# All low parts of the usual experts' weights on VectorE, products by low parts last in a block, and the split's steps at the block's begin and end

## The chip, the cores and the metric

One core of a Trainium2 chip. The engines run their own queues in order and wait for each other by semaphores: TensorE (PE; its weight loads, PEld, overlap its products), VectorE (DVE), ScalarE (ACT), GpSimd (POOL) and the DMA queues, of which SyncE (SP) issues most. The metric is the device time of one execution in microseconds (us).

## The reference

Attention over pooled queries, then two mixtures of experts (MoE), each with 8 experts of which a token takes one:

```python
# attention: 2 batches, 8 heads, 1152 keys, queries averaged in pairs, head size 64
x = softmax(scale * mean_of_pairs(q) @ k.T) @ v            # -> 1152 tokens of 512
# first MoE: expert = argmax(x @ w_gate); an expert takes its first 288 tokens
out[token] = gate * (relu(x[token] @ w1[e]) @ w2[e])       # w1 512x1024, w2 1024x512
# second MoE: tokens with x @ w_skip > 0 only, no limit
out[token] = x[token] + gate * (relu(x[token] @ w1[e]) @ w2[e])
```

All data are float32.

## The kernel before

Attention takes the first 318 us and is left alone by the change, but for its tail. Then come the experts of the first MoE (344 to 519 us), its last block beside the second router (to 565 us), and the experts of the second MoE.

**Split numbers.** For the experts a float32 is split into a high and a low part of twelve bits each (`hi`, `lo` for weights; `xx[:, 0]`, `xx[:, 1]` for tokens; `hh`, `hl` for hidden values), and a product is the sum of three: high by high, high by low, low by high. An expert's weights are 2 x 4096 numbers on each of 128 partitions. `split_ops` returns 17 steps for them: step u casts piece u (512 columns) of `raw` to `hi` on ACT (line 818) and subtracts for piece u-1, `lo = raw - hi` (line 808). The subtraction ran on POOL for the pieces in `ON_POOL`, 6 of 16, and in some splits for further ones (`pool_steps`), else on DVE. After the last piece of a quarter, `load_next` has SP load a quarter of a later expert's weights (1 MB) into the place that came free; for the second half of an expert these loads are issued behind its last chunk (`late`).

**A block.** `block_t` computes one chunk of up to 128 tokens of an expert: `first(0)` (12 products of 128x128 by 128x512, into `ph`), relu on ACT to `hs` (line 942), `first(1)` with the transposes `turn(0)` in its middle (to `pg`; ACT copies to `hh`, line 950; DVE subtracts to `hl`, line 951), `second(py, 0)` with `turn(1)` in its middle, `second(py, 1)`; then DVE scales to `yt` (lines 991, 993), makes an index `ix`, and POOL scatters the rows. Between the parts `flush(list, n)` issues the next n steps of a list: `fill` is the split of the next expert's weights, `preps` the transposes (`psx`, line 913) and the two parts of the next chunks' tokens: `xxn` for the next expert, `xx` for this one's second chunk. A main block is an expert's first chunk; it alone carries `fill`. The second and third chunks stand under conditions (`tc.If`, lines 1172 and 1178) on the count of tokens. An engine that skips them runs a branch and then raises its own semaphore by what the skipped instructions would have added; whoever waits for an instruction from the far side of the condition waits for that. `hs` is written by DVE too, in `block_h` (up to 64 tokens), under a condition.

**Order.** The order of issue on each engine is that of the calls in the code (`manual_schedule`); nothing reorders it. In the first MoE the last expert's main block is left for the end: there `fill` holds five empty steps, then router steps mixed with the split of the second MoE's first expert, whose `hi` and `lo` go to the places of the weights that this block itself uses. Tiles of `wp` have two places each for the halves, in two pools that the experts take in turn.

Of the kernel before, what the change touches and what calls it, by code (L numbers as in the profile page):

```python
# [8 lines left out]
F32 = mybir.dt.float32  # L9
F32R = mybir.dt.float32r  # L10
BF16 = mybir.dt.bfloat16
# [5 lines left out]
P = 128  # L17
# [4 lines left out]
def fused_kernel(  # L22
# [21 lines left out]
    KD = DM // P  # contraction chunks of the first product  # L44
    KF = F // P  # and of the second
    KC = S // P  # key chunks
    QP = 96  # rows of a chunk of queries, as loaded
    QC = SQ // QP
    CH = [P] * (SQ // P) + ([SQ % P] if SQ % P else [])  # token chunks of a batch
    NCH = len(CH)  # L50
    NT = B * NCH
    ROW = DM + 8  # a dispatched row: the token, its gate, its index
    REG = N  # rows of an expert's region
    NPRE = 3  # chunks of an expert that are read without an index
# [8 lines left out]
    # ---------------------------------------------------------------- constants  # L63
# [6 lines left out]
    rev = consts.tile([P, NT, E], F32, name="rev")  # E - e  # L70
# [10 lines left out]
    tri = consts.tile([P, P], BF16, name="tri")  # tri[k, m] = 1 where k < m  # L81
# [9 lines left out]
    def load_small(zeros):  # L91
        """Steps: the routers' weights, the capacity, zeros where tokens may be missing."""
# [22 lines left out]
        def capacity_value():  # L115
            # low + 2^32 * (high + (low < 0)), and not below 0
# [12 lines left out]
    # ---------------------------------------------------------------- weights  # L129
    RW = KD * F // 2  # words of a partition in one load: half of w1[e] or of w2[e]  # L130
# [15 lines left out]
    # ---------------------------------------------------------------- routing  # L146
# [5 lines left out]
    def masks(m):  # L152
        """1 in the rows of an expert's chunks that have no token."""
        nc.vector.tensor_tensor(
            out=mask[m],
            in0=cnt[m].unsqueeze(2).to_broadcast([P, E, NPRE]),
            in1=rowid.unsqueeze(1).to_broadcast([P, E, NPRE]),
            op=ALU.is_le,
        )

    def route(sp, ps_r, lg, nt, gate_out, prev, do=None, half_rows=()):
        """Three steps: the expert of each token, one-hot; its place among that expert's tokens; its gate.

        lg [P, nt, >= E] in SBUF; prev: one-hots of earlier tokens. The dictionary that is returned gets
        the one-hots (oh), the place (rank) and the first row of the expert's region (base).
        """
# [74 lines left out]
    def together(*lists):  # L241
        """The steps of several lists in turn."""
# [6 lines left out]
    def logits(m, rows, lg, ta, tb, xt, lt, groups, on_scalar=lambda j: j and j % 2, j0=0):  # L249
        """Steps to the logits of chunks of 128 tokens: for each group of chunks (each in a quadrant of the  # L250
        partitions) the transposes, the product and the way back."""
# [36 lines left out]
    def in_line(groups):  # L288
        """The steps of logits() in a row, a group's last ones behind the first transpose of the next."""
# [6 lines left out]
    def add_rows(ps, rows, places, first, last):  # L296
        """Adds to ps the transpose of the rows, each in its place: exact, by products with 0 and 1."""
# [10 lines left out]
    def places_of(place, oh):  # L308
        """One-hots of the tokens' places among an expert's first 128."""
# [3 lines left out]
    def count(ps_r, ohs, limit, m):  # L313
        """Tokens of each expert, on every partition, and in row 0 as integers."""
# [11 lines left out]
    def warm(ps, n):  # L326
        """Products that nobody reads: the array's clock would fall while it waits."""
# [24 lines left out]
    # ================================================================ attention  # L352
# [10 lines left out]
    def gate(b, ta, tb, groups):  # L363
        """Routing of a batch's tokens, and their rows to their experts' regions: steps to the logits, and the rest."""
# [31 lines left out]
    with ExitStack() as actx:  # L396
# [16 lines left out]
        PARTS = [(0, 2), (2, NCH)]  # chunks of the two halves of a pair's product with v  # L413
# [24 lines left out]
        def split0(n):  # L438
            """Sums of the pairs of queries, as far as the loads allow ahead."""
# [898 lines left out]
```

## Time and profile before

| | us |
|---|---|
| median of 3 runs | 742.46 |
| the runs | 737.96 to 743.23 |
| span of the profiled execution, first to last instruction | 734.7 |

The profiled execution has no time of its own beside its span; a run counts some us around the span. Shares of busy time are averages over attention, the routers and the experts.

### The profile page before, as it was taken

The numbers are of one execution on the slowest core, as the hardware profiler recorded it, in microseconds if no ns is written. First come the engines' busy times: TensorE is split into PE (matmuls) and PEld (weight loads), VectorE is DVE, ScalarE is ACT, GpSimd is POOL, SyncE is SP. The second block draws the span as 40 slices with busy tenths as digits, with TensorE's granted clock in tenths as the row PEclk, the third lists the DMA queues.
The fourth block names the chain that finished last, engine by engine and source line by source line (L and its number), as shares of the span: only waits on it lengthen the run. The fifth ranks groups of instructions, "written<-read, shape, count | busy, mean of one in ns | idle before, by whom it ended". The sixth has DMA issues, their size and how long they took to land. (4 is left out here: it accounts for less than half of the span.)

```text
span 734.7 us, 11243 instructions
## 1 busy us (share of the span) xinstructions
PE 666.5 (91%) x3978; PEld 485.9 (66%) x3978; DVE 450.1 (61%) x729; ACT 433.3 (59%) x961; POOL 257.3 (35%) x240
## 2 busy tenths in 40 slices
PE   7999999999999999988888998899769888888994
PEld 6766667666767666646666766676648666666673
DVE  5755656565656664564888548842175788888211
ACT  5876767676757676651777347722350677776210
POOL 4322222222222520053566226510165566665010
PEclk8999999999999999999999999999988999999998
DMA  6042624050202122033889618850454798884100
GB/s 179 31 138 104 212 104 167 17 196 17 81 17 82 67 71 78 16 123 114 302 314 331 246 35 311 278 201 19 147 186 147 259 318 303 315 302 162 32 30 13
DMA packets 55599, 111.39 MB, mean 152 GB/s; under 512 B 5470, under 2 KB 14686, under 8 KB 55488
## 3 DMA queue, kind: packets, MB, share of 16 engines
q1 hardware_dynamic: 52128, 102.27, 40.8%
q0 software_dynamic: 3360, 7.72, 2.8%
q8 instruction: 59, 0.97, 0.5%
q14 instruction: 52, 0.43, 0.2%
HBM read 93.51 MB, written 19.71 MB: 154 GB/s over the span
## 5 line engine op out<-in xcount | busy, mean ns | idle before, releaser
L808 POOL TENSOR_TENSOR lo<-raw,hi 128x512 fp32r<-128x512 f32 x101 | 142.0, 1409 | 115.6 <-ACT hi L818 113.2
L808 DVE TENSOR_TENSOR lo<-raw,hi 128x512 fp32r<-128x512 f32 x155 | 157.2, 1065 | 4.3 <-ACT hi L818 4.3
L818 ACT CAST hi<-raw 128x512 fp32r<-128x512 f32 x256 | 141.5, 626 | 0.6 <-PE py L958 0.6
L527 PE MATMUL s_ps<-kop,qop 128*128 128x384 f32 x480 | 125.5, 369 | 1.7 <-ACT a L571 1.4
L555 DVE TENSOR_REDUCE m<-s_ps 128x1 f32<-128x1152 f32 x72 | 97.7, 1357 | 24.6 <-PE s_ps L527 22.4
L601 PE MATMUL pt<-ident,a 128*128 128x128 f32 x648 | 109.8, 283 | 3.2 <-ACT kop L476 1.1
L571 ACT ACTIVATE a<-s_ps,m 128x384 f32<-128x384 f32 (+1 forms) x144 | 106.8, 747 | 3.1 <-DVE m L555 2.9
L476 ACT COPY at<-pt 128x384 f32<-128x384 f32 x144 | 68.2, 481 | 64.0 <-PE pt L601 63.9
L601 PEld LDWEIGHTS pt<-ident,a 128*128 128x128 f32 x648 | 71.5, 140 | 45.9 <-ACT at L476 13.0
L627 PE MATMUL pv<-at,vr 128*64 128x320 f32 (+1 forms) x576 | 97.9, 428 | 0.0
L938 PE MATMUL ph<-hi,xxn 128*128 128x512 f32 x224 | 77.1, 405 | 13.1 <-PEq L1172 10.4
L476 DVE COPY at<-pt 128x384 f32<-128x384 f32 x72 | 39.8, 553 | 76.2 <-PE pt L601 74.1
L951 DVE TENSOR_TENSOR hl<-pg,hh 128x512 fp32r<-128x512 f32 x42 | 28.9, 687 | 89.0 <-ACT hh L950 89.0
L958 PE MATMUL py<-hi,hl 128*128 128x512 f32 x168 | 67.8, 404 | 12.5 <-DVE hl L951 12.5
L942 ACT ACTIVATE hs<-ph 128x512 f32<-128x512 f32 x42 | 25.1, 598 | 91.0 <-PE ph L938 52.3
L527 PEld LDWEIGHTS s_ps<-kop,qop 128*128 128x128 f32 x480 | 75.1, 187 | 5.3 <-ACT a L571 3.8
L958 PE MATMUL py<-hi,hh 128*128 128x512 f32 x168 | 68.7, 409 | 0.6
L886 POOL DMA_INDIRECT out_dram<-yt,ix x23 | 22.6, 981 | 133.0 <-DVE ix L883 81.7
L958 PE MATMUL py<-lo,hh 128*128 128x512 f32 x168 | 67.7, 403 | 0.0
L466 POOL TENSOR_TENSOR qhl<-qr,qhl 96x384 fp32r<-96x384 f32 x30 | 29.9, 1016 | 95.7 <-DVE qhl L464 95.7
L938 PEld LDWEIGHTS ph<-hi,xxn 128*128 128x128 f32 x224 | 42.1, 188 | 27.3 <-ACTq L1172 12.1
L454 POOL TENSOR_TENSOR khl<-kr_None,khl 128x576 fp32r<-128x576 f32 x14 | 19.8, 1414 | 87.2 <-DVE khl L453 87.2
(170 smaller groups left out, 948.2 us busy)
## 6 DMA issues: line engine op xcount, KB each, us to landing
raw<-in_moe_w_dram SPq DMA_DIRECT2D x64, 1024.0 KB, 6.0
x<-xs SPq DMA_DIRECT2D x36, 260.0 KB, 6.3
xs<-xtok SPq DMA_DIRECT2D x8, 780.0 KB, 7.4
qr<-in_q_dram SPq DMA_DIRECT2D x16, 288.0 KB, 3.2
vr<-in_v_dram SPq DMA_DIRECT2D x8, 576.0 KB, 6.0
kr_None<-in_k_dram SPq DMA_DIRECT2D x7, 576.0 KB, 5.0
out_dram<-xtok SPq DMA_DIRECT2D x3, 768.0 KB, 7.7
x<-out_dram SPq DMA_DIRECT2D x4, 512.0 KB, 6.3
```

The lines of the kernel that those rows point to most:

```text
L466: sub.tensor_tensor(out=t[:, 1, :, r, :], in0=qs, in1=t[:, 0, :, r, :].bitcast(F32), op=ALU.subtract)
L476: (nc.vector.tensor_copy if on_vector else nc.scalar.copy)(dst, src)
L527: i = nc.tensor.matmul(s_ps[0:M, bank[j], 0 : 3 * P], qop[n + r][:, part, o : o + M], kop[n + r][:, j, :], start=(part == 0 and r == (c == ...
L555: i = nc.vector.tensor_reduce(out=nm, in_=s_ps[:, lo : lo + 3, 0 : 3 * P], axis=AX.XY, op=ALU.max, negate=True)
L571: i = nc.scalar.activation(a[:, a0 : a0 + nb, :], s_ps[:, b0 : b0 + nb, 0 : 3 * P], AF.Exp, bias=nm, accum_out=t[:, c, n % 2, k : k + 1],)
L601: nc.tensor.transpose(ps[:, x * P : (x + 1) * P], a[:, g, x * P : (x + 1) * P], ident)
L627: nc.tensor.matmul(hold["pv"][j * D : (j + 1) * D, 0:w], vrt[i][:, j, c * D : (c + 1) * D], at_t[2 * i + j, part][:, c, :], start=(c == 0) ...
L808: eng.tensor_tensor(out=lo, in0=raw, in1=hi.bitcast(F32), op=ALU.subtract)
L818: nc.scalar.copy(hi, raw)
L938: lambda d=d, i=i, a=a, b=b: nc.tensor.matmul(ps, xx[:, a, d, :], w1[b][:, d, s], start=(d + i == 0), stop=(d == KD - 1 and i == 2))
L951: nc.vector.tensor_tensor(out=hl[:, fs, :], in0=ps, in1=hh[:, fs, :].bitcast(F32), op=ALU.subtract)
L958: lambda f=f, i=i, a=a, b=b: nc.tensor.matmul(py, a[:, f, :], w2[b][:, f, :], start=(f + i == 0), stop=(f == KF - 1 and i == 2))
```

## The change

1. `ON_POOL` goes. Low parts are on DVE but for `pool_steps`: pieces 13 to 15 of the very first split and 8, 9, 10, 13, 14 of the second MoE's first. The other 14 splits have none on POOL.
2. In `block_t` the loops of `first` and `second` are exchanged: four products high by high, four high by the weights' low part, four low by high, where it was three for each of four pieces.
3. The 17 steps of `fill` are spread as 4 ahead of `first(0)`, then 2, 1, 1, 2, 3 and the rest (4), where it was 2, 3, 2, 2, 3 and the rest (5).
4. Comments are removed; lines behind 788 move up by one to the flush that is added in `block_t`.

```diff
-        NU = 16  # steps of a split
-        ON_POOL = (0, 3, 6, 8, 11, 14)  # those whose low parts GpSimd takes
+        NU = 16
...
-                eng = nc.gpsimd if u in ON_POOL or u in pool_steps else nc.vector
+                eng = nc.gpsimd if u in pool_steps else nc.vector
...
-                for d in range(KD):
-                    for i, (a, b) in enumerate(((0, 0), (0, 1), (1, 0))):
+                for i, (a, b) in enumerate(((0, 0), (0, 1), (1, 0))):
+                    for d in range(KD):
                         mms.append(
...
-                for f in range(hf * 4, hf * 4 + 4):
-                    for i, (a, b) in enumerate(((hh, 0), (hh, 1), (hl, 0))):
+                for i, (a, b) in enumerate(((hh, 0), (hh, 1), (hl, 0))):
+                    for f in range(hf * 4, hf * 4 + 4):
                         mms.append(
...
+            flush(fill, 4)
             mms, relu = first(0)
             flush(mms, 12)
             relu()
             flush(fill, 2)
             mms, relu = first(1)
             flush(mms, 6)
             turn(0)
-            flush(fill, 3)
+            flush(fill, 1)
             flush(mms, 12)
             relu()
-            flush(fill, 2)
+            flush(fill, 1)
             py = pa([P, DM], "py")
             mms = second(py, 0)
             flush(mms, 6)
             turn(1)
             flush(preps, 1)
             flush(fill, 2)
             flush(mms, 12)
             mms = second(py, 1)
             flush(fill, 3)
             flush(mms, 4)
             flush(preps, 1)
             flush(fill, len(fill))
             flush(mms, 12)
```

DVE in the second expert's main block (`lo_2_*` is the split for the third expert, `hl` the hidden values' low part, `xx` a second chunk's), before:

```order
L951 TENSOR_TENSOR hl<-pg,hh 128x512
L808 TENSOR_TENSOR lo_2_0_4385<-raw_2_0_0_3895,hi_2_0_4384 128x512 x2
L808 TENSOR_TENSOR lo_2_0_4385<-raw_2_0_1_3933,hi_2_0_4384 128x512 x2
L951 TENSOR_TENSOR hl<-pg,hh 128x512
L918 TENSOR_TENSOR xxn<-psx,xxn 128x512
L808 TENSOR_TENSOR lo_2_0_4385<-raw_2_0_1_3933,hi_2_0_4384 128x512
L808 TENSOR_TENSOR lo_2_1_4387<-raw_2_1_0_4380,hi_2_1_4386 128x512 x2
L918 TENSOR_TENSOR xx_4393<-psx,xx_4393 128x512
L808 TENSOR_TENSOR lo_2_1_4387<-raw_2_1_1_4382,hi_2_1_4386 128x512 x3
L991 TENSOR_SCALAR yt<-py,x_1_0_3841 128x512
```

and now:

```order
L807 TENSOR_TENSOR lo_2_0_4385<-raw_2_0_0_3881,hi_2_0_4384 128x512 x4
L807 TENSOR_TENSOR lo_2_0_4385<-raw_2_0_1_3933,hi_2_0_4384 128x512
L950 TENSOR_TENSOR hl<-pg,hh 128x512
L807 TENSOR_TENSOR lo_2_0_4385<-raw_2_0_1_3933,hi_2_0_4384 128x512 x2
L950 TENSOR_TENSOR hl<-pg,hh 128x512
L917 TENSOR_TENSOR xxn<-psx,xxn 128x512
L807 TENSOR_TENSOR lo_2_0_4385<-raw_2_0_1_3933,hi_2_0_4384 128x512
L807 TENSOR_TENSOR lo_2_1_4387<-raw_2_1_0_4380,hi_2_1_4386 128x512 x4
L917 TENSOR_TENSOR xx_4393<-psx,xx_4393 128x512
L807 TENSOR_TENSOR lo_2_1_4387<-raw_2_1_1_4382,hi_2_1_4386 128x512 x4
L991 TENSOR_SCALAR yt<-py,x_1_0_3841 128x512
```

Five low parts stand ahead of the first `hl`, two between the two `hl` where there were four, and nine behind the second where there were six.

PE from the second transposes of the same block on (`lo_1_1` is the low part of this expert's second weights), now; before, `hi,hh`, `lo,hh` and `hi,hl` followed each other product by product, in the same places around `pg` and `psx`:

```order
L957 MATMUL py<-hi_1_1_3847,hh 128x512 x4
L957 MATMUL py<-lo_1_1_3848,hh 128x512 x2
L947 MATMUL pg<-ident,hs 128x128 x4
L912 MATMUL psx<-ident,x_2_0_3849 128x128 x4
L957 MATMUL py<-lo_1_1_3848,hh 128x512 x2
L957 MATMUL py<-hi_1_1_3847,hl 128x512 x4
L957 MATMUL py<-hi_1_1_3847,hh 128x512 x4
L912 MATMUL psx<-ident,x_1_1_3851 128x128 x4
L957 MATMUL py<-lo_1_1_3848,hh 128x512 x4
L957 MATMUL py<-hi_1_1_3847,hl 128x512 x4
```

The products that read `hl` moved from third to ninth in each half.

ACT in the last block of the first MoE (`hi_0_0_8738` is the first half of the second MoE's first expert, `gx` a router's transposes), before:

```order
L942 ACTIVATE hs<-ph 128x512
L950 CAST hh<-pg 128x512
L942 ACTIVATE hs<-ph 128x512
L818 CAST hi_0_0_8738<-raw_0_0_0_6697 128x512 x2
L950 CAST hh<-pg 128x512
L261 COPY xT_0_8802<-gx_0_8797 128x512
```

and now:

```order
L941 ACTIVATE hs<-ph 128x512
L817 CAST hi_0_0_8738<-raw_0_0_0_6683 128x512
L949 CAST hh<-pg 128x512
L817 CAST hi_0_0_8738<-raw_0_0_0_6683 128x512
L941 ACTIVATE hs<-ph 128x512
L261 COPY xT_0_8788<-gx_0_8783 128x512
L949 CAST hh<-pg 128x512
```

A cast that waits for PE moved from behind the second `hs` to between the first `hs` and the first `hh`.

## Rows read from the trace of the kernel before

**Rows 1.** The page's first lines: span, then busy us (share) xinstructions

```profile
span 734.7 us, 11243 instructions
...
PE 666.5 (91%) x3978; PEld 485.9 (66%) x3978; DVE 450.1 (61%) x729; ACT 433.3 (59%) x961; POOL 257.3 (35%) x240
```

**Rows 2.** PE's waits from 344 us on: engine, line, releaser; us, times, longest

```profile
PE py L958 <- DVE hl L951: 12.5, 13, 1.4
...
PE pr L214 <- DVE oh L198: 6.0, 2, 5.7
```

**Rows 3.** Timeline of PE, a main block: start us, us, what, [idle before <-releaser]

```profile
446.70 0.47 PE L938 MATMUL ph<-hi,xxn 128*128 128x512 f32 x1 [1.01 <-PEq L1172]
...
450.98 0.60 PE L948 MATMUL pg<-ident,hs 128*128 128x128 f32 x4
...
456.93 0.40 PE L958 MATMUL py<-lo,hh 128*128 128x512 f32 x1
458.25 0.51 PE L958 MATMUL py<-hi,hl 128*128 128x512 f32 x1 [0.92 <-DVE hl L951]
...
462.42 0.47 PE L938 MATMUL ph<-hi,xxn 128*128 128x512 f32 x1 [1.13 <-PEq L1172]
```

**Rows 4.** Timeline of DVE, the same block

```profile
449.04 0.74 DVE L991 TENSOR_SCALAR yt<-py,x 128x512 f32<-128x512 f32 x1
...
452.28 0.69 DVE L951 TENSOR_TENSOR hl<-pg,hh 128x512 fp32r<-128x512 f32 x1 [2.43 <-ACT hh L950]
452.89 4.70 DVE L808 TENSOR_TENSOR lo<-raw,hi 128x512 fp32r<-128x512 f32 x4
457.51 0.68 DVE L951 TENSOR_TENSOR hl<-pg,hh 128x512 fp32r<-128x512 f32 x1
```

**Rows 5.** Timeline of ACT, the same block

```profile
450.02 0.60 ACT L942 ACTIVATE hs<-ph 128x512 f32<-128x512 f32 x1 [3.49 <-DVEq L1172]
450.51 1.13 ACT L818 CAST hi<-raw 128x512 fp32r<-128x512 f32 x2
...
455.22 0.60 ACT L950 CAST hh<-pg 128x512 fp32r<-128x512 f32 x1
```

**Rows 6.** Line 808: engine, operation, count, ns min/median/max, first and last start

```profile
L808 DVE TENSOR_TENSOR lo<-raw,hi x155: 674/681/1806, 318.0 to 677.9; 128x512 fp32r<-128x512 f32 x155
L808 POOL TENSOR_TENSOR lo<-raw,hi x101: 1252/1317/1830, 317.5 to 675.5; 128x512 fp32r<-128x512 f32 x101
```

**Rows 7.** Timelines of DVE, then of POOL, around 448 us

```profile
447.83 1.28 DVE L808 TENSOR_TENSOR lo<-raw,hi 128x512 fp32r<-128x512 f32 x2
...
450.12 0.99 POOL L886 DMA_INDIRECT out_dram<-yt,ix  x1 [2.76 <-DVEq L1172]
```

**Rows 8.** Timeline of PE at the head of two second chunks

```profile
408.25 0.74 PE L938 MATMUL ph<-hi,xx 128*128 128x512 f32 x2 [0.60 <-DVE xx L918]
...
676.20 0.68 PE L1036 MATMUL ph<-hi,xx 128*64 128x512 f32 x2 [0.61 <-DVE xx L918]
```

**Rows 9.** Timeline of PE in attention's tail

```profile
319.84 0.41 PE L653 MATMUL px<-ident,xu 128*128 128x128 f32 x2 [1.60 <-DVE xu L637]
```

**Rows 10.** Timeline of ACT in the last block of the first MoE

```profile
525.35 0.59 ACT L950 CAST hh<-pg 128x512 fp32r<-128x512 f32 x1 [1.45 <-PE pg L948]
526.70 0.60 ACT L942 ACTIVATE hs<-ph 128x512 f32<-128x512 f32 x1 [0.77 <-PE ph L938]
```

**Rows 11.** Timeline of DVE in the second router

```profile
539.27 5.45 DVE L1236 TENSOR_SCALAR do<-lg 128x5 f32<-128x5 f32 x1
```

**Rows 12.** Timeline of POOL in the second router

```profile
539.77 4.92 POOL L808 TENSOR_TENSOR lo<-raw,hi 128x512 fp32r<-128x512 f32 x4
```

**Rows 13.** Two blocks: stretch, us, busy per engine, PE clock, DMA share, GB/s

```profile
377.13:391.84 14.71, 13.63 (x64) 10.38 (x65) 12.21 (x15) 10.84 (x21) 8.74 (x7) 1.00 0.95 332
629.47:645.07 15.60, 13.66 (x64) 10.40 (x65) 13.02 (x17) 11.52 (x22) 9.30 (x8) 1.00 0.92 308
```

**Rows 14.** The page's DMA issues: queue, count, size, median us to landing

```profile
raw<-in_moe_w_dram SPq DMA_DIRECT2D x64, 1024.0 KB, 6.0
```


## Prediction

> **What bounds the kernel now.** I read the page first: TensorE (PE) is busy in 91% of the span [rows 1], so only what makes it wait can pay. The change touches the experts, so I listed PE's waits from 344 us on [rows 2]. At the top stand 13 waits, 12.5 us in all, of the second product for `hl`, the low part of the hidden values that VectorE (DVE) makes. There is one in 13 of the 14 main blocks that also split the next expert's weights; the fourteenth, the first of all, doesn't have it.
>
> One such block in order of time [rows 3 to 5], with 0 at its first product (446.70): 18 products take 4.28 us, 0.24 each; the second transpose gives `hh` at +8.5, done at +9.1; `hl` needs only that, but starts at +10.8, because DVE is still at low parts of weights. PE issues a product at 456.93 and the next at 458.25: 1.32 us where 0.24 is usual, so a stall costs 1.08.
>
> Why is DVE late? A low part takes 674 ns at the least, 681 in the median and 1806 at the most on DVE, 1317 on GpSimd (POOL) [rows 6]. The two lows at 447.83, while POOL stands still (it idles 2.76 us up to 450.12), take 1.28 us together, 0.61 from start to start [rows 7]; the four from 452.89, with POOL at the same kind of work, 4.70 [rows 4]. So the six steps that POOL takes off DVE are paid by DVE in the others. At the start of a block DVE idles 2.43 us before the first `hl` [rows 4] and ACT 3.49 us before `hs` [rows 5]: there is room where the change puts the steps.
>
> **The change part by part.** My sum is made against the profiled execution, whose span is 734.7 us [rows 1]; the runs stand at 738.0 to 743.2, so 3 to 9 us lie around the span, and I take the differences off the median, 742.46.
>
> *Low parts on DVE, 16 of an expert in place of 10.* 16 times 0.61 is 9.8 us; four of `hl` and `xx` at 0.61, and 0.98 from the start of `yt` to the `hs` that waits for the branch behind it [rows 4, 5], make 13.2 in a block that lasts 15.72 now: it fits. Where it lies decides. From `hh` at +9.1 DVE now has `hl`, the `xx` of the next block, five lows, `xx` of the second chunk, four lows: 12 steps of 0.61, 7.3 us, so `yt` at +16.4. `hl` is ready at +9.8. In the new order of products it is wanted six products and one set of transposes later than before: +10.5 plus 1.4 plus 0.4, +12.3. There are 2.5 us of room, and the stall goes. All 13: 12.5 us of idle, and 0.16 each of lost pace (1.08 less 0.92), **-14.6**.
>
> *What is late next.* `hs` of a block's first half waits for DVE to be through its tail and the branch: in the block shown ACT's 3.49 us end on DVE's branch, 0.98 us after the start of `yt` [rows 4, 5]. In the new order that is +17.4, and the next block starts at 15.72 - 1.08 = +14.6, so `hs` could go at +2.8. PE's first 12 products end at about +3.1, and the transposes want `hs` (0.6 long) by +4.28, so it may start as late as +3.7. It is hidden with 0.9 us to spare; what is queued behind `hs` on ACT (`hi` casts, `hh`) has the same room. A slip beyond costs PE one for one. I put **+1.0** for all blocks, 0 to +6.
>
> [...] The trace has the next low start 0.61 us after the one before, while one is recorded as 0.68 long [rows 6, 7]. [...]
>
> *The order of products.* Their number and that of weight loads stays. The low part of the tokens (`xx`, on DVE) is wanted by the ninth product instead of the third. It made PE wait 0.60 and 0.61 at the head of two second chunks [rows 8]; six products are 1.4 us, both waits go: **-1.2**. A gain is bounded by these two rows, a loss I see none: low parts of weights were needed second, now fifth.
>
> *Casts at the begin, on ACT.* Four `hi` casts (two take 1.13 us [rows 5], four about 2.2) now stand ahead of `hs`, in the 3.49 us that ACT idled. They need PE to be through with the expert before, which is so at the block's start, and the load of the weights, below. Nothing as long as they end by +3.7: they end at +2.2.
>
> *The first split, in attention's tail.* Five low parts move from POOL to DVE. PE waited 1.60 us for `xu` there [rows 9], which stood behind one low beside POOL's; now it stands behind two at 0.61. Between +0.6 (one low more in the way) and -1.6 (the wait gone) I take the middle, **-0.5**.
>
> *The last block of the first MoE.* It runs with the split of the second MoE's first expert, whose places are those of its own weights. A placeholder list kept these steps behind the first product; with four steps flushed at the begin the first cast now stands between `hs` and `hh` on ACT and waits for PE to end the first product. `hh` ran at 525.35 and the second half's `hs`, which follows that end, at 526.70 [rows 10]. The cast goes at 526.7 and `hh`, 0.5 behind it, at 527.2, 1.85 later than now, done at 527.8. PE stands still from the first product's end, just before 526.7, less some 0.4 that a group of four router transposes, moved ahead, fills (four took 0.60 with their overlap [rows 3]). **+1.0**, from 0 (other waits hide it) to +1.9.
>
> *The second router.* A tiny DVE step, `do`, takes 5.45 us [rows 11], as long as POOL's four lows in a row at 539.77, 4.92 us [rows 12]; PE stands 5.7 us behind it [rows 2]. One of the four (step 11) goes to DVE, behind this chain: 4.92/4 = 1.2 less, and 0.6 on DVE later. **-0.6**, from -1.2 to +0.6.
>
> Loads: they are started when a quarter's low parts are done; none is added. Scatters on POOL start earlier in the queue and nothing waits for them inside a block.
>
> Sum: -14.6 + 1.0 - 1.2 - 0.5 + 1.0 - 0.6 = -14.9, so 742.46 - 14.9 = 727.6, rounded to 727.5. **I forecast 727.5 us.**
>
> **The rivals.**
>
> *Half of it comes (0.17, 734).* The stall goes, but another pace takes over. The DMA engines are busy 92% of 15.60 us in one block, 14.4 us; another ran 14.71 us at 95%, 14.0 [rows 13]. A block of 14.6 would have them at 96 to 98%, and whatever they can't follow PE gives back. For it: hardly any slack. Against: 95% was held without PE waiting for a weight. At 0.6 us back in each of 13 blocks, +7, so 734.
>
> *A slower kernel: `hs` behind casts that wait for weights (0.06, 752).* The first cast moves from +3.8 to 0. Its quarter is loaded when the fourth low is done, at about +2.9 + 4 x 0.61 = +5.3 of the block before, 9.3 us ahead of the cast; a load takes 6.0 us from issue to landing in the median [rows 14]. The casts may slip to +1.5, so loss starts at a landing of 10.8 us; every us more costs 13 us, and from 12.0 on the gain is eaten. At 12.7 it is 727.5 + 25 = 752. For it: the engines near 96%. Against: it needs double the present landing.
>
> *It doesn't do what it says (0.07, 741).* What holds DVE up may be more than POOL. If lows come 0.77 us apart with POOL silent, 16 x 0.77 + 3.4 = 15.7 fills the present block and DVE sets its length; then the head waits and a little more are left, -1 to -2. Against: 674 ns at the least, 681 in the median, and 0.61 from start to start [rows 6, 7].
>
> *DVE steps don't overlap (0.03, 729).* If each step waits for the recorded end of the last, 12 x 0.07 = 0.9 us puts `hs` at +3.7, just at its limit; 0.1 in each of 13 blocks on the sum as it stands, 729. [...] Against: the starts in rows 7.
>
> **How the numbers follow.** The forecast has 0.67. About 1%, 7.4 us, is what a measurement of this kernel tells from no change (its three runs spread over 5.3): the bounds are 735.0 and 749.9. Faster: nearly all of 0.67, the 0.03, and a little over a third of the half case, 0.76. Same: the rest of the half case, the 0.07 and some of the forecast's edge, 0.17. Slower: 0.07. The range: best case -14.6 - 1.2 - 1.6 + 0 - 1.2 is -18.6, 723.9, and a run at the low edge of the spread, 4.5 lower, 719; upward the half case with its spread to 738. What lies outside is the 0.07 at 741, the 0.06 and a few hundredths below.
>
> **What the new profile would show.** Right: POOL's lows fall from 101 to 8, DVE's rise to 248 with a mean near 0.68 us; no PE wait for `hl`; main blocks without a second chunk at about 14.6 us from start to start; `hs` still ended by DVE's branch, near +2.8; the last block of the first MoE about 1 us longer at `hh`. Wrong if PE waits for `hs` in most blocks, if ACT waits for `raw` at the first cast, if DMA stands at 100%, or if DVE's lows stay at 1 us.

## The result, and the profile after

| | median, us | runs, us | ratio to the kernel before, 95% interval |
|---|---|---|---|
| kernel before | 742.85 | 737.96 to 743.39 (4) | |
| changed kernel | 716.66 | 712.63 to 723.73 (4) | 0.965 [0.961, 0.970] |

The changed kernel is faster by 3.5%, 26 us. I had forecast 727.5 us, 15 us less, with a range from 719 to 738: the direction was right, the gain too small, and the time lies under the range. The ratio leaves out the slowest of the four runs, which is over 1.5% above the fastest; in e8 below the same kernel ran from 715.60 to 724.46 us.

The profiled execution is shorter by 19.6 us (734.7 before [rows 1]). The page's first lines, span and then busy time of each engine:

```profile
span 715.1 us, 11137 instructions
...
PE 660.8 (92%) x3978; PEld 487.7 (68%) x3978; DVE 446.7 (62%) x822; ACT 436.1 (61%) x961; POOL 128.4 (18%) x147
```

POOL went from 35% to 18%. TensorE's (PE's) waits from 344 us on (engine, line, releaser; us in total, times, longest), which answer to [rows 2]:

```profile
PE ph L937 <- PEq L1172: 8.0, 6, 1.9
PE pr L214 <- DVE oh L198: 5.3, 2, 4.4
PE ph L937 <- PEq L1188: 4.6, 1, 4.6
PE ph L937 <- issue: 3.5, 3, 1.7
PE psx L912 <- DMA x<-xs: 2.4, 2, 1.8
...
PE py L957 <- ACT hh L949: 0.8, 1, 0.8
```

The 13 waits for `hl` are gone. The head of the list is a wait of which I had taken little notice before: the first product of a block, released by PE's own sequencer at line 1172, the branch over the second chunk. Before it stood at 10.4 us in 8 places.

Line 807, the low parts (count, ns min/median/max), against [rows 6]:

```profile
L807 DVE TENSOR_TENSOR lo<-raw,hi x248: 659/681/757, 317.4 to 658.0; 128x512 fp32r<-128x512 f32 x124
...
L807 POOL TENSOR_TENSOR lo<-raw,hi x8: 1255/1277/2111, 326.0 to 545.3; 128x512 fp32r<-128x512 f32 x8
```

All as forecast: 248 on DVE, 8 on POOL. The median on DVE is what it was, 681 ns, but the slowest takes 757 ns where it took 1806. The median hides the change: before, the 38 low parts on DVE beside which POOL subtracted nothing took 679 ns in the mean and 685 at the most, the other 117 took 1191 in the mean; now the mean of all is 684.

Where the time went by stage: the three stretches of blocks that carry a split, before (stretch, us, busy time per engine, PE clock, DMA share, GB/s):

```profile
344.18:407.02 62.84, 54.97 (x256) 41.59 (x257) 52.37 (x63) 44.89 (x87) 38.95 (x29) 1.00 0.84 296
431.19:476.83 45.64, 40.73 (x193) 31.24 (x192) 36.38 (x45) 34.15 (x66) 26.97 (x20) 1.00 0.69 235
565.34:674.96 109.62, 95.96 (x449) 72.64 (x450) 88.92 (x111) 79.47 (x153) 66.34 (x50) 1.00 0.83 285
```

and after:

```profile
342.36:401.77 59.41, 53.12 (x257) 42.29 (x258) 50.92 (x87) 46.06 (x87) 5.72 (x6) 1.00 0.90 315
425.04:466.14 41.10, 39.57 (x194) 31.55 (x192) 36.60 (x63) 35.03 (x66) 5.49 (x3) 1.00 0.77 266
554.82:655.62 100.80, 94.46 (x449) 74.83 (x450) 88.82 (x153) 80.94 (x153) 7.86 (x9) 0.98 0.88 310
```

62.84 + 45.64 + 109.62 = 218.10 us became 59.41 + 41.10 + 100.80 = 201.31: -16.8 us, where the prediction had -14.6 + 1.0 = -13.6 (stalls and `hs`). This is one execution of each kernel: in the profiled executions of e4 and e8 below, again of the kernel before and of the changed one, the same stretches took 217.5 and 209.9 us, which is -7.6. The DMA engines, busy 0.84, 0.69 and 0.83 of the time, went to 0.90, 0.77 and 0.88.

One of these blocks after, PE with start, length and what (its predecessor in [rows 3] is 446.70 to 462.42):

```profile
438.31 1.18 PE L937 MATMUL ph<-hi,xxn 128*128 128x512 f32 x4
...
445.88 0.60 PE L947 MATMUL pg<-ident,hs 128*128 128x128 f32 x4
...
450.45 1.10 PE L957 MATMUL py<-hi,hl 128*128 128x512 f32 x4
452.92 0.93 PE L937 MATMUL ph<-hi,xxn 128*128 128x512 f32 x3 [1.37 <-PEq L1172]
```

and DVE in the same block:

```profile
438.54 2.48 DVE L807 TENSOR_TENSOR lo<-raw,hi 128x512 fp32r<-128x512 f32 x4
...
447.13 0.69 DVE L950 TENSOR_TENSOR hl<-pg,hh 128x512 fp32r<-128x512 f32 x1 [0.17 <-ACT hh L949]
```

With 0 at 438.31, `hl` starts at +8.82, 2 us earlier than before (+10.81), and the product that reads it at +12.14, without a wait. The products end without a stall, and still the next block starts only at +14.61, behind 1.37 us of idle time. This block is as long as I had forecast (+14.6) for another reason than I had given; its neighbours take 13.27 and 13.22 us.

### The profile page after: what moved, and what is told of

Its sections match the earlier page's. It is cut to its first block, busy times and chain, and to the rows that moved or that the text cites. A ratio compares the mean times of both kernels' runs of the same rounds, so it can differ in the third digit from the quotient of the medians.

```text
span 715.1 us, 11137 instructions
## 1 busy us (share of the span) xinstructions
PE 660.8 (92%) x3978; PEld 487.7 (68%) x3978; DVE 446.7 (62%) x822; ACT 436.1 (61%) x961; POOL 128.4 (18%) x147
## 5 line engine op out<-in xcount | busy, mean ns | idle before, releaser
L807 DVE TENSOR_TENSOR lo<-raw,hi 128x512 fp32r<-128x512 f32 x248 | 155.6, 684 | 6.3 <-ACT hi L817 3.8
L817 ACT CAST hi<-raw 128x512 fp32r<-128x512 f32 x256 | 143.0, 623 | 8.4 <-PEq L1172 4.0
L885 POOL DMA_INDIRECT out_dram<-yt,ix x23 | 24.9, 1084 | 285.7 <-DVEq L1172 149.1
L937 PE MATMUL ph<-hi,xxn 128*128 128x512 f32 x224 | 61.5, 406 | 13.2 <-PEq L1172 8.0
L957 PE MATMUL py<-lo,hh 128*128 128x512 f32 x168 | 52.5, 414 | 0.0
L957 PE MATMUL py<-hi,hh 128*128 128x512 f32 x168 | 46.7, 399 | 1.3 <-ACT hh L949 0.8
L627 PEld LDWEIGHTS pv<-at,vr 128*64 128x64 f32 x576 | 30.0, 135 | 23.8 <-issue 18.3
L957 PE MATMUL py<-hi,hl 128*128 128x512 f32 x168 | 46.0, 395 | 0.0
L949 ACT CAST hh<-pg 128x512 fp32r<-128x512 f32 x42 | 24.6, 587 | 29.6 <-PE pg L947 27.7
```

The lines of the kernel that those rows point to most:

```text
L627: nc.tensor.matmul(hold["pv"][j * D : (j + 1) * D, 0:w], vrt[i][:, j, c * D : (c + 1) * D], at_t[2 * i + j, part][:, c, :], start=(c == 0) ...
L807: eng.tensor_tensor(out=lo, in0=raw, in1=hi.bitcast(F32), op=ALU.subtract)
L817: nc.scalar.copy(hi, raw)
L885: i = nc.gpsimd.indirect_dma_start(out=out, out_offset=bass.IndirectOffsetOnAxis(ap=ix[:M], axis=0), in_=yt[:M], in_offset=None, bounds_ch ...
L937: lambda d=d, i=i, a=a, b=b: nc.tensor.matmul(ps, xx[:, a, d, :], w1[b][:, d, s], start=(d + i == 0), stop=(d == KD - 1 and i == 2))
L957: lambda f=f, i=i, a=a, b=b: nc.tensor.matmul(py, a[:, f, :], w2[b][:, f, :], start=(f + i == 0), stop=(f == KF - 1 and i == 2))
```

## Where a block's length comes from

Beside the waits the profile has the branch itself. In the block of [rows 3] before (line, engine's queue, operation, count, ns, start):

```profile
L1172 PEldq COMPARE_BRANCH  x1: 3833/3833/3833, 458.4 to 458.4; - x1
```

It starts at 458.4, 0.2 us behind the end of the second `hl` (457.51 + 0.68 [rows 4]), and lasts 3.83 us; 0.17 us behind its end the next block's first product starts, at 462.42. ACT's same branch takes 45 ns in the median, DVE's 56. PE's sequencer runs ahead of the products here: once `hl` is there, nothing in the block makes it wait, and it comes to the branch while PE still has 2.9 us of products to do (they end at 461.29). So the chain of such a block is

the second `hl` ends, +0.2, the branch (3.4 to 4.3 us before, where it fetches code), +0.17, the next block: 11.49 + 0.22 + 3.83 + 0.17 = 15.71 us, which is the block's length.

The stall of 1.08 us and the idle time at the branch were two faces of one lateness (e2 and e9 below show it). Two branches of the changed kernel, of the block above and of a later one:

```profile
L1172 PEldq COMPARE_BRANCH  x1: 4873/4873/4873, 447.9 to 447.9; - x1
...
L1172 PEldq COMPARE_BRANCH  x1: 3355/3355/3355, 623.9 to 623.9; - x1
```

The first starts at +9.57: 9.51 + 0.06 + 4.87 + 0.17 = 14.61. The second takes 3.36 and ends 12.90 us into its block (614.38), under products that last 13.38: no gap. What makes a branch this long is the traffic on the DMA engines (e12 shows it by taking the loads away: the longest of these branches lasts 3.70 us there, 5.44 in the changed kernel). Two stretches of the first branch, from its start and from 2.45 us on (queue: packets, MB, share of the engines):

```profile
q1 hardware_dynamic: 227, 0.85, 85.4%
...
q1 hardware_dynamic: 67, 0.25, 70.0%
q8 instruction: 1, 0.02, 5.8%
```

The packet of queue 8 is 16 KB of instructions. For 2.45 us of this branch none was moved (the first stretch lists no queue 8), while the weight loads had the engines 85% busy; then the packet took 0.98 us, and 1.58 us later the first product ran. In the second branch the packet started 0.99 us behind the branch. Not every jump brings a packet: two of the eleven before (at 388.82 and 656.77) brought none, took 0.43 and 0.41 us, and PE did not wait. So the time of a long branch goes with its packet: the nine that brought one took 3.36 to 4.27 us, and the first product came 1.52 to 1.73 us behind the landing. PE's five branches into a second chunk brought none either and took 70 to 78 ns.

## The experiments

All ratios are to runs of the kernel before on the same chip; its medians there were 736.7 to 738.4 us. The groups e1 to e4, e5 to e8, e9 to e11 and e12 to e15 ran on four different chips, so what compares between groups is the ratio. "Before" and "after" in the edits are the two kernels.

| run | edit | median, us | ratio, 95% interval |
|---|---|---|---|
| e1 | before, low parts on DVE | 723.29 | 0.980 [0.976, 0.985] |
| e2 | before, order of products | 741.53 | 1.006 [1.003, 1.009] |
| e3 | before, places | 737.98 | 1.000 [0.997, 1.003] |
| e4 | before | 735.40 | 0.998 [0.995, 1.001] |
| e5 | e1 and order | 721.14 | 0.977 [0.974, 0.981] |
| e6 | e1 and places | 721.92 | 0.979 [0.975, 0.982] |
| e8 | after | 719.71 | 0.975 [0.971, 0.979] |
| e9 | after, second transposes later | 721.94 | 0.980 [0.975, 0.985] |
| e10 | after, second transposes earlier | 731.12 | 0.989 [0.984, 0.995] |
| e11 | e10 and two empty steps more | 731.88 | 0.987 [0.982, 0.993] |
| e14 | after, loads in halves | 723.13 | 0.981 [0.977, 0.985] |
| e15 | e10, loads in halves | 731.42 | 0.990 [0.987, 0.993] |

e7, e12 and e13 compute something else (below), and their times don't compare.

**e1, the low parts alone.**

```diff
-        ON_POOL = (0, 3, 6, 8, 11, 14)
+        ON_POOL = ()
```

> The kernel before, only with no low part on GpSimd but those of pool_steps. Theory 1 (GpSimd's subtractions beside VectorE's are what makes the low parts and hl late): the low parts on VectorE come at 0.68 us, hl of the second half is done near +9.8 of a block and wanted at +10.6, the 13 waits for hl go, -14 us; the waits at the heads of two second chunks stay, so about 728 us. Theory 2 (what matters is when hl is wanted, the order of products): five low parts stand between the two hl instead of four, the waits stay and the time is within 4 us of before.

Measured 723.29 us, 14.2 under the 737.45 of the kernel before beside it: theory 1's direction, and with -14 us even its size, but not its way there. PE's waits:

```profile
PE ph L938 <- PEq L1172: 18.2, 10, 2.7
PE pr L214 <- DVE oh L198: 6.0, 2, 4.4
PE ph L938 <- PEq L1188: 4.0, 1, 4.0
```

No wait for `hl` is left, as expected, and the wait at the branch is 18.2 us in 10 places instead of 10.4 in 8. One of its branches:

```profile
L1172 PEldq COMPARE_BRANCH  x1: 5053/5053/5053, 451.0 to 451.0; - x1
```

The second `hl` ends at +9.88 here; 9.88 + 0.22 + 5.05 + 0.17 = 15.32, the length of this block (440.90). With the old places a weight load is issued 2.0 us ahead of the branch, and the code starts to come 2.2 to 3.3 us behind it in nine of ten branches (0.9 to 1.5 before, where the load mostly came 3.1 us ahead). So of what `hl` gained in this block, 1.61 us, all but 0.4 was lost to the longer branch. Five blocks of the second MoE, first before and then in e1 (stretch, us, busy, clock, DMA share, GB/s):

```profile
582.69:659.79 77.10, 68.28 (x320) 51.97 (x321) 63.39 (x78) 56.84 (x109) 46.02 (x34) 1.00 0.88 305
```

```profile
576.46:653.73 77.27, 69.97 (x320) 54.60 (x321) 61.80 (x107) 55.94 (x108) 4.90 (x5) 0.96 0.89 307
```

They gained nothing, and all stretches with a split took 214.3 us for 218.1. This profiled execution is the slowest of the six, 730.06 us; the others, at 721 to 725 us, must have gained more, and no trace shows where.

**e2, the order of products alone.**

```diff
-                for d in range(KD):
-                    for i, (a, b) in enumerate(((0, 0), (0, 1), (1, 0))):
+                for i, (a, b) in enumerate(((0, 0), (0, 1), (1, 0))):
+                    for d in range(KD):
```

and the same in `second`.

> The kernel before, only with the products by low parts last. Theory 1: the waits for hl go too, since hl at +11.4 is wanted at +12.0, but ten low parts of 1.1 to 1.2 us and the rest of VectorE's work are 14.5 to 15.4 us, so VectorE sets the length of a block: of 1.1 us a block a third comes, -4 to -6 us, 737 to 739, and the waits turn up at hs. Theory 2: the waits for hl go and nothing takes their place, -14 us, and both head waits go, about 727 us.

Slower by 0.6%. Both theories were wrong: theory 2 wholly, theory 1 in the sign. The waits:

```profile
PE ph L938 <- PEq L1172: 20.6, 9, 4.2
...
PE py L958 <- DVE hl L951: 0.8, 1, 0.8
```

The products no longer wait for `hl` (0.8 us of some 12), and nothing is won, because `hl` comes when it came before and the branch with it: +11.50 + 0.06 + 3.89 + 0.17 = 15.62 in the block at 445.23. The stall only moved to the branch, where it is one long gap, mostly of 2.1 to 2.4 us, and with seven of the eight gaps of 2.05 us or more PE's granted clock falls to half (0.50; not behind the 2.09 us ahead of the block at 445.23). Five blocks (stretch, us, busy, clock):

```profile
581.44:665.85 84.41, 75.80 (x321) 58.92 (x321) 60.74 (x75) 55.94 (x108) 47.91 (x34) 0.88 0.78 278
```

at a mean granted clock of 0.88, and the head of one of them:

```profile
599.51 1.18 PE L938 MATMUL ph<-hi,xxn 128*128 128x512 f32 x4 [2.05 <-PEq L1172]
600.52 1.56 PE L938 MATMUL ph<-lo,xxn 128*128 128x512 f32 x4
601.88 2.34 PE L938 MATMUL ph<-hi,xxn 128*128 128x512 f32 x5
```

Product by product, the trace has the first ones 0.23 to 0.31 us from start to start (0.24 is usual), and from the seventh on 0.43: the granted clock has fallen. It is 0.78 in the mean from 599.51 to 602.00 and 0.92 from there to 616.60, which 3.4 us at 0.50 and the rest at 1.00 would give. The first 12 take 4.1 us instead of 2.88, and the block 17.1.

**e3, the places alone,** with POOL's share as before.

```diff
+            flush(fill, 4)
             mms, relu = first(0)
...
-            flush(fill, 3)
+            flush(fill, 1)
...
-            flush(fill, 2)
+            flush(fill, 1)
```

> The kernel before, only with the split's steps at the new places. Theory 1: two low parts instead of four lie between the two hl, hl is on time, but VectorE is as full as with the old places and hs falls behind its tail: -2 to -6 us, 737 to 741 us, with waits for hs. Theory 3 (the places alone make the change): -14 us, 728. For the last block of the first MoE: 1 us more at hh, as forecast.

No change, 1.000: the upper end of theory 1. DVE's low parts are still slowed (up to 4.7 us for one), and the waits for `hl` stay in half of the blocks, beside those at the branch:

```profile
PE ph L938 <- PEq L1173: 9.7, 6, 3.3
PE py L958 <- DVE hl L951: 9.0, 7, 3.5
```

**e4, the kernel before again,** without an edit.

> The kernel before as it is, to see why its runs stand at 738 to 743 us and its profiled execution at a span of 734.7, when the runs of the changed kernel stand 1.9 us above their spans. Theory of the execution: 1.9 us lie around the span here too, and what differs between executions is TensorE's granted clock: spans of 736 to 741.5 us at mean clocks of 0.978 down to 0.970. Theory of the overhead: 3 to 9 us lie around a span that stays near 735.

The theory of the execution holds in its first part: every run stands 1.8 to 1.9 us above its span (732.2 and 734.04 in the profiled one). The mean clock goes along with the time only in part: the 12 runs spread from 732.72 at 0.987 to 740.53 at 0.975, but 735.22 is at 0.979 and 737.20 at 0.983. All but two of the 62 further runs of the kernel before lie between 733.8 and 742.9 us, with medians near 737.5. The median of the three runs that I was shown, 742.46, stood some 5 us above that, and the profiled execution (734.7 + 1.9 = 736.6) did not.

**e5 and e6, pairs:** the edit of e1 with that of e2, and with that of e3.

> Low parts on VectorE and the products by low parts last, but the split's steps at their old places. The branch theory (what sets a main block without a second chunk is the second hl, then 0.1 us, then TensorE's branch over the skipped chunk with its code fetch, then 0.17 us): the second hl ends at +9.9 as in e1, the fetch still waits for the load that is issued 2 us ahead of the branch, so the blocks stay at 15 us; only the waits for xx go: 1 to 2 us under e1, 720 to 723 us. The theory of the prediction (stalls of hl and xx alone): the same as the changed kernel, within 2 us of it.

> Low parts on VectorE and the split's steps at the new places, but the old order of products. The branch theory: the second hl ends at +9.5 as in the changed kernel and the loads are issued as there, so the blocks take 13.3 to 15 us as there; the branch starts 0.2 us behind hl, not 0.06, and the xx waits at two second chunks may stay: 0 to 3 us over the changed kernel. A theory that the order of products carries the further gain: as e1, 7 us over the changed kernel.

Both times are where the branch theory had them, 1.4 and 2.2 us over e8, but they don't decide: e5 also lies within 2 us of the changed kernel, as the other theory had it, and the intervals of e1, e5, e6 and e8 overlap. The traces tell more. In e5 a load is issued 1.8 us ahead of the branch, the fetch starts 2.4 to 2.5 us behind it in six of nine, and five of those blocks take 14.9 us (the sixth 16.45). In e6 the loads are mostly issued 4.4 us ahead of the branch (3.3 to 4.9 in most blocks of the changed kernel), the fetch mostly starts 0.9 to 1.4 us behind it, and the blocks are shorter. Five blocks, first in e5 and then in e6:

```profile
574.25:648.98 74.73, 68.53 (x321) 53.50 (x321) 61.84 (x107) 55.89 (x108) 4.89 (x5) 0.98 0.92 316
```

```profile
572.50:643.70 71.20, 67.36 (x321) 52.30 (x321) 62.68 (x107) 57.86 (x110) 4.92 (x5) 1.00 0.95 335
```

They take 70.7 us in the changed kernel, 72.2 in e8 and 77.3 in e1. So, in one execution of each, it is more the places than the order that shorten these blocks behind e1; by the times alone no gain beyond that of e1 is shown.

**e8, the changed kernel again,** without an edit.

> The changed kernel as it is, on the chip of these runs, where the kernel before ran at 734 to 742 us: if the ratio of 0.965 holds, 710 us; if the kernel before was slow by its chip or its executions at first, 716 to 718 us, a ratio of 0.972.

719.71 us, a ratio of 0.975, the second case: some 18 us, not 26, is what the change is worth against the kernel before at its usual time. The two intervals, [0.961, 0.970] and [0.971, 0.979], don't touch. Of the difference of 7.9 us, 4.9 lie in the kernel before (742.85 and 737.97) and 3.1 in the changed one; why stays open. For the second part the trace of e8 (723.24 us, span 721.3) gives a lead. Two of its blocks take 17.75 and 19.57 us, the same two 15.05 and 15.66 in the first profile, and these 6.6 us are about the 6.2 between the spans. One waited 3.10 us for code in the middle of a block, the other 4.49 at a branch whose fetch started 3.9 us late: the changed kernel's time depends on when its code comes, and that differs between executions.

**e7 and e12, no loads of weights.** In e1's kernel and in the changed one:

```diff
         seq_at[0] += 1
+        if seq_at[0] > 4:
+            raw_t[m, e, half, r] = raw_t[0, 0, half, r]
+            return
```

> As e1, but with no loads of weights behind the first expert's: every expert computes with the first one's weights. The branch theory, with the fetch of TensorE's code held up by the loads: with idle DMA engines the fetch starts 0.95 us behind the branch instead of 2.2 to 3.3, the branch takes 3.3 us instead of 4.6 to 5.6, and the ten main blocks go from 15.0 us to 13.6 to 13.8, their bound by products: 12 to 15 us under e1, 708 to 711 us. If the loads don't matter to the branch, the blocks stay at 15 us and the time within 3 us of e1.

> The changed kernel with no loads of weights behind the first expert's (every expert computes with the first one's, which also changes what the second router sends where, so blocks are compared and not totals). If the loads alone delay the code: the fetch starts 0.9 to 1.1 us behind every branch, the branch takes 3.3 to 3.8 us, no gap over 0.5 us is left and the main blocks take 13.2 to 13.6 us where they take 13.2 to 15.1. If something else does, fetches at +1.8 to +2.9 and blocks of 14 to 15 us stay.

In e7 the fetch started 0.90 to 1.06 us behind each of 11 branches, and they took 3.35 to 3.80 us, as expected; the blocks took 13.8 to 15.1, not 13.6 to 13.8, because `hs` now waited for DVE's tail (4.0 us in 8 places). Its time, 680.9 us, says nothing, since other second chunks are run. In e12 (line 1175 is 1172) one branch, and the DMA engines while its code comes (first the busy tenths in 40 slices, then the queue):

```profile
L1175 PEldq COMPARE_BRANCH  x1: 3656/3656/3656, 586.6 to 586.6; - x1
```

```profile
DMA  0900000000000000000000000000000000000000
...
q8 instruction: 1, 0.02, 5.6%
```

The code is the only packet in this stretch. Five blocks of the second MoE:

```profile
563.71:630.67 66.96, 66.21 (x321) 52.42 (x321) 63.19 (x108) 57.77 (x110) 7.41 (x5) 1.00 0.15 45
```

13.39 us each, without a gap over 0.2 us at a branch (behind the first block of each MoE it is 1.3 to 1.6). The changed kernel with its loads:

```profile
570.48:641.15 70.67, 67.65 (x321) 53.70 (x321) 63.74 (x109) 57.91 (x110) 4.88 (x5) 0.98 0.96 339
```

These are 14.13 us each. So it is the loads that delay the code, and they cost the changed kernel about 0.7 us a block, what the clock lost in one block (586.90, below) included. The theory is shown by this edit: a jump that fetches takes 3.1 to 3.8 us without any load, and what is beyond is the loads'.

**e9 and e10, the second `hl` moved.** In `block_t` of the changed kernel, with 10 in e9 and 4 in e10:

```diff
             mms = second(py, 0)
-            flush(mms, 6)
+            flush(mms, 10)
             turn(1)
```

> The changed kernel, only with the second transposes (and by them the second hh and hl) four products later, behind the tenth product of their half. The products that read them still stand behind them by 0.3 us or more, so no product waits. The branch theory: hl ends 0.94 us later, the branch starts 0.94 us later, and each main block without a second chunk is longer by the part of it that isn't hidden under products, 0.5 to 0.94 us; with ten such blocks +5 to +9 us, 724 to 729 us, all of it in waits for the branch. The prediction's view (a wait for hl costs only where a product stands at it, the gap at a branch is TensorE's own): no change, 718 to 721 us.

> The changed kernel, only with the second transposes two products earlier, behind the fourth product of their half; hs is ready 0.1 us ahead of them. The branch theory: the branch starts 0.47 us earlier and the blocks in which its fetch is late give back up to that, some seven of ten: -2 to -4 us, 715 to 718 us. The prediction's view: no change, 718 to 721 us.

e9 is 2.2 us over e8, with intervals that overlap: less than the branch theory expected, and by the time alone it can't be told from no change. The profile tells. A block of e9 with a fetch on time (branch 3.28 us) and one of the changed kernel (3.54):

```profile
589.50 1.18 PE L937 MATMUL ph<-hi,xxn 128*128 128x512 f32 x4 [0.68 <-PEq L1172]
```

```profile
600.49 0.71 PE L937 MATMUL ph<-hi,xxn 128*128 128x512 f32 x2
```

The later `hl` gave 0.68 us of idle time at the branch where there was none (0.67 or more at each of nine branches); no product waits for `hl`. Its size was missed because the fetches came sooner behind the later branch (0.8 to 1.5 us in eight of nine; 1.0 to 2.9 in the changed kernel); the loads had mostly been issued 4.2 us or more ahead of it.

e10 fell on the other side of my expectation: 731.12 us, 11 us over e8. The second `hl` ends 0.47 us earlier, as meant (+8.99), but the branch starts mostly at +9.34, only 0.2 us earlier, 0.35 behind the end of `hl`: here `hl` is no longer what it waits for (what is stays open), and the edit tests the branch theory badly. Ten blocks take 13.3 to 14.9 us. The loss sits in the other four: the first of each MoE (21.57 and 19.63 us, 16.45 and 15.66 in the changed kernel's first profile) and the ones ahead of a second chunk (18.44 and 17.18, 15.05 and 14.47). They wait for what comes by DMA, for rows of tokens in the former and for code in the middle of a block in the latter:

```profile
PE ph L937 <- issue: 7.3, 3, 3.8
...
PE psx L912 <- DMA x<-xs: 6.1, 2, 4.0
```

```profile
396.36 2.08 PE L937 MATMUL ph<-hi,xxn 128*128 128x512 f32 x4 [3.85 <-issue]
```

The code for this product came from 393.92 to 394.97, 1.4 us ahead of it. These are the waits that e8 has too: there the four blocks take 16.43, 17.75, 19.57 and 14.70 us. In e10 they are together 8.4 us longer than in e8, and the spans differ by 8.1 (729.4 and 721.3).

**e13, e14 and e15, what e10 waited for.** e13 is e10 with the edit of e12; e14 and e15 are the changed kernel and e10 with each load of 1 MB cut in two (twice as many places, each of half the size):

```diff
-    RW = KD * F // 2
+    RW = KD * F // 4
...
-    seq = [... for half in range(2) for r in range(2)]
+    seq = [... for half in range(2) for r in range(4)]
```

> As e12, with the second transposes two products earlier (e10). If e10 lost its time to code and token rows that wait behind the loads: the three long blocks of e10 (20.3, 18.4 and 17.2 us) are gone, no wait for a token row or for code over 1 us is left in them, and the main blocks take 13.2 to 13.5 us, as in e12. If the order of e10 itself is at fault, the three blocks stay longer than in e12 by 2 us or more.

> The changed kernel with each load of 1 MB cut into two of 512 KB, each started when its own half of the low parts is done; the bytes are the same. If small transfers wait for what is queued ahead of them: half as much is queued, the fetch behind a branch starts 0.5 to 1 us sooner where it was late, the waits for code inside blocks shrink, -3 to -6 us, 712 to 717 us. If only the sum of bytes counts (the DMA engines are busy 96% of five main blocks): no change, 717 to 721 us.

> As e14, with the second transposes two products earlier. If e10 lost its time behind the 1 MB loads, half of its 10 us come back and the earlier branch gives its 2 us: 712 to 724 us. If not, 729 to 732 us as in e10.

In e13 the three blocks that the expectation names take 14.02, 13.05 and 13.37 us (14.56, 13.09 and 13.39 in e12); the fourth, the first of the second MoE, 16.56 (16.06 in e12). So the loads are the cause; the order alone makes no block long. Cutting the loads helps neither kernel: 723.13 us (0.981, beside 0.975 of e8) and 731.42, with code that started to come up to 3.7 us behind a branch. The size of a piece isn't what delays the code; that the sum of bytes is, fits this and is not shown. Why these four blocks wait longer in e10 than in e8 stays open.

**e11, the last block of the first MoE.** e10 with

```diff
-        last_block([lambda: None] * 5 + ...
+        last_block([lambda: None] * 7 + ...
```

> As e10, and with seven empty steps in place of five ahead of the split in the last block of the first MoE, so that no cast that waits for TensorE stands between hs and hh. If the term of the prediction holds (the cast costs about 1 us there): another 0.7 to 1.3 us less than e10, TensorE's 0.75 us wait for hh gone, 714 to 717 us.

PE's wait of 0.75 us for `hh` is gone, but the stretch to the second MoE takes 45.21 us against 45.18 in e10, and the time, 731.88 us, is e10's: no gain is seen. One execution of each can't exclude a small one, since the changed kernel has 46.05 us for this stretch in one execution and 45.41 in the other.

No version beat the changed kernel.

## Why the prediction was right and wrong, step by step

*Why `hl` was late: right.* POOL's subtractions slow DVE's: before, beside them, a low part took 1191 ns in the mean, without them none takes over 757, four take 2.48 us (0.60 from start to start), and by the medians e1 alone has 14.2 of the 18.3 us of e8. The rival of steps that come 0.77 us apart fell, and so did that of steps that don't overlap: the next low part starts 0.60 us after the start of one that is 0.68 long.

*What a stall is worth: the step that failed.* I took 1.08 us a stall and let the next block start "at 15.72 - 1.08 = +14.6", with the idle time at the branch as PE's own and fixed. It was the end of a chain from the same `hl`: 0.2 us, a branch of 3.4 us or more, 0.17 us. By it the end of `hl` at +9.5 instead of +11.5 is worth 2.0 us to a block, until the products (13.4 us) take over or a fetch is late: blocks of 13.2 to 15.1 us, and -16.8 us where I had -13.6 with the term for `hs`. In e4 and e8 it is -7.6, with two blocks of the changed kernel held up by late code, so the size is shown less well than the mechanism. e2 shows that removing the stall alone is worth nothing, so that the sum of the stalls came near the truth was luck.

*The base: the other step that failed, and the larger part of the miss.* I subtracted from the median, 742.46, and held 3 to 9 us for what lies around the span. 1.9 us lie around it; the rest was the shown runs' excess over the profiled execution. From 736.6 the same sum gives 721.7, 2 us over e8 and 5 us over the first result. Of the 10.8 us that the forecast missed, 5.9 are this base (742.46 - 736.6), and 4.7 are what the trace of the first result has beyond the sum (19.6 - 14.9).

*`hs` behind DVE's tail: 1.0 us forecast, 0 measured.* `hs` starts at +3.0 to +3.8 where a block has no long wait in it, in time for the transposes; no wait for it is in the list. DVE's branch ends its wait in three blocks, at +3.6, not in most and at +2.8; elsewhere it is PE's products.

*The casts and the waits for weights:* only 0.2 us of waiting for a cast turned up, in one block. The rival of a slower kernel had no part.

*The heads of two second chunks: right.* They start without a wait; the two chunks are 0.89 and 0.56 us shorter, -1.45 for -1.2.

*Attention's tail.* The wait [rows 9] went from 1.60 to 1.02 us:

```profile
319.12 0.41 PE L653 MATMUL px<-ident,xu 128*128 128x128 f32 x2 [1.02 <-DVE rs L642]
```

The experts begin 1.8 us earlier than in the profile of before, but at 342.4 in e4 too. Over the kept executions with all weight loads they begin at 342.4 to 344.2 us with the old share of POOL and at 340.8 to 343.8 with the new one: the size of this term, forecast as -0.5, is not settled.

*The last block of the first MoE.* The cast stands where I put it and PE waits 0.75 us for `hh`, but e11, without that wait, is not faster: nearer to 0, the lower bound, than to the +1.0 that I took.

*The second router: right in kind and size of its first part.* `do` and the POOL steps ahead of it:

```profile
530.03 4.21 DVE L1236 TENSOR_SCALAR do<-lg 128x5 f32<-128x5 f32 x1
```

```profile
530.50 3.70 POOL L807 TENSOR_TENSOR lo<-raw,hi 128x512 fp32r<-128x512 f32 x3
```

4.21 us for 5.45, three low parts for four, and PE's wait 4.4 for 5.7. With the last block, the whole stretch takes 46.05 us for 46.50: -0.45, where both terms gave +0.4 (46.10 in e4 and 45.41 in e8, -0.7).

*The rival in which the DMA engines set the pace* came true in part. They are busy 96% of the five blocks from 570.48 on, no product waits for a weight, and yet the loads take their 0.7 us a block, through the code. Its sum had a slip: 13 times 0.6 is 7.8, not 7, so its time was 735.

## What to carry to other kernels

When a wait's releaser is the engine's own sequencer at a branch, ask when the branch began and for what the sequencer had waited before it: that value, and not the stall at the product that reads it, can be what sets the loop, as the second `hl` did here: 0.2 us from its end to a branch of 3.83, 0.17 from there to the next block. A gain there is the shift of the last awaited value up to the next bound, not the sum of the stalls. Subtract a sum that is made from one execution from that execution's own time, and carry the result to other runs as a ratio.

## What the runs showed of the hardware

- PE's branch over a skipped second chunk, where it fetched code, took 3.1 to 3.9 us without the weight loads (e7, e12, e13) and up to 6.9 us with them (e11). Its 16 KB of code took about 1 us (0.93 to 1.72 before), and the first product came 1.5 to 1.7 us behind their landing where they landed late. The two jumps of the kernel before for which no code came took 0.4 us.
- In straight code PE waited for code too, under the loads (the DMA engines 96% busy in five blocks of the changed kernel): it stood 3.85 us in the middle of a row of products in e10, and 1.74 and 1.27 us in the changed kernel (3.1 in e8), each time with 16 KB of code that landed 1.2 to 1.4 us ahead of the next product. In e12 and e13, without the loads, there is no such wait.
- PE's granted clock can fall behind a gap at the branch. In the changed kernel PE was idle 1.93 us up to 585.60, and from 586.9 on ran at half, a granted clock of 0.50:

```profile
586.90:590.20 3.30, 3.30 (x9) 2.54 (x8) 2.93 (x6) 0.98 (x3) 0.98 (x1) 0.50 1.05 383
```

The first 12 products of that block took 4.19 us for 2.88. It isn't so behind each such gap: before, one of 2.52 us was followed by 12 products in 2.89.
